# The attention state of the first twelve tiles: added on TensorE through an identity and copied by ScalarE instead of added on VectorE, with the first loads in another order

## The chip, the cores and the metric

The kernel runs on one core of a Trainium2 chip. Its time is the device time of one execution in microseconds (us), and the smaller is the better. Five engines work side by side, each through its own queue in order: TensorE (PE in the rows, its weight loads PEld), VectorE (DVE), ScalarE (ACT), GpSimd (POOL) and SyncE (SP), which issues nearly all transfers (DMA).

## The reference

Three layers, one after the other, on 3072 tokens of 512 channels. The change lies in the first.

```python
# attention: B=4 sequences, H=8 heads, S=768, head size 64
state = zeros((B, H, D, D))
for t in range(S):
    state = gamma * state + k[:, :, t] (outer) v[:, :, t]
    y[:, :, t] = scale * q[:, :, t] @ state
# x = y as (3072, 512)
h = x @ w_in;  x = (max(h, 0) + alpha * min(h, 0)) @ w_out      # dense layer, 2048 wide
# expert layer: 8 experts of 1024; each token goes to one expert
out[t] = gate[t] * (max(x[t] @ w1[e], 0) @ w2[e])
```

The inputs are float32, and the result has to be about that exact. The kernel therefore splits operands into two float16 halves (high and low) and multiplies with three products, or it multiplies in float32.

## The kernel before

**Tiles.** The 3072 tokens are 24 tiles of 128: tile `i` is chunk `c = i // 4` of sequence `b = i % 4`. The recurrence is done by chunks: within a tile by masked scores, across tiles by a state per sequence. The state lies in `st_bd[:, b]`, as four 128x128 blocks of which only the two 64x64 blocks on the diagonal are used; the rest stays at zero from a memset.

**What one tile does** (lines 476 to 610):

- `att_load` issues the loads on SP's queue: `qk_t[i]` (q, k by channel and k by token, 768 KB), `v_t[i]` (256 KB), and for every fourth tile the decay factors `cqk_sb` of its chunk (512 KB: one half for q, one for k).
- `att_hat` multiplies q (and, for tiles from `HALVED = 12` on, k) by the factors on VectorE. For tiles below 12 only the q half of `cqk_sb` is read, and v is scaled instead of k.
- `att_a` makes the scores on TensorE in float32, and VectorE masks them with `cau`.
- `att_b` multiplies scores by v and q by the state into the PSUM bank `y`, then k by v into the PSUM bank `u` (128x512), both in float32 for tiles below 12. ScalarE sums the squares of `y`, VectorE derives a scale, ScalarE and VectorE write the two halves `xh`. Last, two VectorE additions (64x256 each) add the diagonal blocks of `u` into `st_bd`. The last chunk of a sequence needs no state.

`y` and `u` come from `m_ring`, which has two banks, handed out in the order of the program; the small sums over partitions (`total`) take their bank from it too.

**The first stretch** also has to prepare the dense layer: `convert` unpacks `w_in` and `w_out` (three ScalarE and two VectorE operations of 1024 columns for each of sixteen pieces), `quarter` and `split_out` split them in halves, and `mm1` / `mm2` multiply. `mm1(0, m)`, the first batch of four tiles, starts as soon as quarter 0 of `w_in` is split, so it is mixed with tiles 4 to 11 and with the rest of the unpacking. Each `mm1` takes a bank of `h_ring` (two) that ScalarE and VectorE empty into `g` and from there into two float16 halves.

**The order of work.** No engine's order is written by hand. Every instruction is recorded by `Plan` (lines 97 to 323) with an estimated duration from `cost`, and `issue` runs a list scheduler over the record: it decides from the estimates in which order each engine, and SP's transfers, get their instructions. All instructions are then emitted by line 147, which is why all rows name that line. Changing an estimate can move instructions on any engine, in the whole kernel.

Of the kernel before, what the change touches and what calls it, by code (L numbers as in the profile page):

```python
# [14 lines left out]
AF = mybir.ActivationFunctionType  # L15
ALU = mybir.AluOpType
AX = mybir.AxisListType

B, H, S, D = 4, 8, 768, 64
NT, DM, DFF = B * S, H * D, 2048  # L20
E, F = 8, 1024
P = 128
# [74 lines left out]
class Plan:  # L97
# [37 lines left out]
    class Engine:  # L135
# [26 lines left out]
        def cost(self, method, kw):  # L162

            n = 1
            for d in kw["out"].shape[1:]:
                n *= d
            if "dma" in method:
                side = kw["in_"] if "indirect" not in method or kw["in_offset"] is None else kw["out"]
                n = 1
                for d in side.shape:  # L170
                    n *= d
                nb = n * mybir.dt.size(side.dtype)
                if "indirect" in method:
                    return 1040.0, 650.0, nb
                return 60.0, (1150.0 if "transpose" in method else 1000.0), nb * (1.23 if "transpose" in method else 1)
            if self.name == "PE":
                if kw["lhsT"].dtype == F32:
                    return max(214.0, 1.67 * n), 0.0, 0
                return max(27.0, 0.416 * n + 2.5), 0.0, 0
            if self.name == "ACT":  # L180
                extra = sum(93.0 for k in ("accum_out", "scale", "bias") if isinstance(kw.get(k), bass.AP))
                return (95.0 if kw["in_"].space != bass.MemoryType.PSUM else 50.0) + 0.833 * n + extra, 0.0, 0
            if self.name == "DVE":
                fast = method in ("tensor_scalar", "tensor_copy") and n > 64 and kw.get("op0") not in self.BITS
                two = method in ("scalar_tensor_tensor", "tensor_tensor") and n > 256
                return 65.0 + n * (0.52 if fast else 1.05) * (1.15 if two else 1.0), 0.0, 0
            return 140.0 + (2.13 if method == "tensor_tensor" else 1.3) * n, 0.0, 0
# [139 lines left out]
def retention_prelu_moe_kernel(ctx: ExitStack, tc, qkv, w_in, w_out, alpha, emb, tau, w1, w2,  # L327
# [3 lines left out]
    V, A, G, T, SP = plan.vector, plan.scalar, plan.gpsimd, plan.tensor, plan.sync  # L331
# [10 lines left out]
    def buf(name, shape, dt=F32):  # L342
        return sbuf.tile([P, *shape], dt, name=name, tag=name)
# [12 lines left out]
    def tmp(name, shape, dt=F32, n=2):  # L356
        if name not in small:
            small[name] = Ring([buf(f"{name}_{k}", shape, dt) for k in range(n)])
        return small[name].next()
# [2 lines left out]
    cst = buf("cst", [NCOL])  # L362
    cst16 = buf("cst16", [2 * P + E], F16)
    cau = buf("cau", [P])
    alpha_sb = buf("alpha_sb", [KF])
    tau_sb = buf("tau_sb", [1])
    cqk_sb = buf("cqk_sb", [2, KD, P])

    def col(name):
        return cst[:, _COLS[name][0]:_COLS[name][1]]  # L370

    tri, ones16, base16 = cst16[:, 0:P], cst16[:, P:2 * P], cst16[:, 2 * P:]
# [14 lines left out]
    v_ring = Ring([vp_buf[:, k] for k in range(2)])  # L387
# [4 lines left out]
    first = {"qk": [room[:, 1536 * k:1536 * k + 1536].rearrange("p (a x) -> p a x", a=3) for k in range(3)] + [qk_buf, hat_buf, stage[:, 12:15]],  # L392
             "v": [room[:, 4608 + 512 * k:5120 + 512 * k] for k in range(2)] + v_ring.bufs,
             "pm": [room[:, 5632 + 512 * k:6144 + 512 * k].rearrange("p (k t) -> p k t", k=KD) for k in range(4)] + pm_ring.bufs,
             "xh": [room[:, 7680 + 512 * k:8192 + 512 * k].bitcast(F16).rearrange("p (a x) -> p a x", a=2) for k in range(3)] + xh_ring.bufs,
             }
    first = {k: Ring(v) for k, v in first.items()}
# [28 lines left out]
    def pow2(ss, s, c, hb=None):  # L426

        if hb is None:
            hb = tmp(f"hb{ss.shape[1]}", [ss.shape[1]], I32)
        V.tensor_scalar(out=hb, in0=ss.bitcast(I32), scalar1=0x7F000000, scalar2=1,  # L430
                        op0=ALU.bitwise_and, op1=ALU.logical_shift_right)
        V.tensor_scalar(out=s.bitcast(I32), in0=hb, scalar1=-1, scalar2=c << 23, op0=ALU.mult, op1=ALU.add)
        return hb

    def pow2_inverse(hb, i, c):
        V.tensor_scalar(out=i.bitcast(I32), in0=hb, scalar1=(254 - c) << 23, scalar2=None, op0=ALU.add)
# [9 lines left out]
    def square_sum(src, acc, junk):  # L446
        A.activation(out=junk, in_=src, func=AF.Square, accum_out=acc)
# [25 lines left out]
    N_ROOM = 2  # L473
    qk_t, v_t, att = {}, {}, {}

    def att_load(i):
        if i % B == 0:
            SP.dma_start(out=cqk_sb, in_=cqk[i // B])
        qk_t[i] = (first["qk"] if i < B * N_ROOM else qk_ring).next() if i < HALVED else qk_buf
        SP.dma_start(out=qk_t[i], in_=qkv[i, :, 0:3])  # L480
        v_t[i] = (first["v"] if i < B * N_ROOM else v_ring).next()
        SP.dma_start(out=v_t[i], in_=qkv[i, :, 3])

    def att_hat(i):
# [40 lines left out]
    HALVED = 12  # L525
# [36 lines left out]
    def att_b(i, early=False):  # L562

        c, b = divmod(i, B)
        j, o = divmod(i, BT)
        v = v_t.pop(i)
        hat, pr = att.pop(i)
        st = st_bd[:, b]
        y = m_ring.next()
        with plan.unit("PE"):  # L570
            for p in range(KD):
                for r in range(2):
                    h = 2 * p + r
                    if i >= HALVED:
                        for n, (a, o_) in enumerate(((0, 0), (0, 1), (1, 0))):
                            T.matmul(out=y[:, D * h:D * h + D], lhsT=p16[r][:, a, P * p:P * p + P],
                                     rhs=v16[:, o_, D * h:D * h + D], start=(r == n == 0), stop=False, skip_group_check=True)
                        continue
                    T.matmul(out=y[:, D * h:D * h + D], lhsT=pr[r][:, p, :], rhs=v[:, D * h:D * h + D],
                             start=(r == 0), stop=(r == 1 and not c), skip_group_check=True)  # L580
                if c:
                    T.matmul(out=y[:, P * p:P * p + P], lhsT=hat[:, 0, P * p:P * p + P], rhs=(st_y if i >= HALVED else st)[:, p, :],
                             start=False, stop=True, skip_group_check=True)
        if c < NCH - 1:
            u = m_ring.next().rearrange("p (k t) -> p k t", k=KD)
            with plan.unit("PE"):
                for p in range(KD):
                    T.matmul(out=u[:, p, :], lhsT=hat[:, 2, P * p:P * p + P], rhs=v[:, P * p:P * p + P],
                             start=True, stop=True)
        xh = (first["xh"] if i < B * N_ROOM else xh_ring).next()  # L590
        ss = tmp("ssx", [1])
        square_sum(y, ss, xh[:, 0, :])
        if c < NCH - 1:
            for r in (0, D):
                V.tensor_tensor(out=st[r:r + D, :, r:r + D], in0=u[r:r + D, :, r:r + D],
                                in1=st[r:r + D, :, r:r + D], op=ALU.add)
        s = tmp("sx", [1])
        pow2(ss, s, C_WIDE, hbx[:, i:i + 1])
        if o == BT - 1:
            pow2_inverse(hbx[:, i + 1 - BT:i + 1], invx[:, i + 1 - BT:i + 1], C_WIDE)  # L600
            for k in range(i + 1 - BT, i + 1):
                if k in y_inv:
                    for q in range(2):
                        V.tensor_tensor(out=invx[:, k:k + 1], in0=invx[:, k:k + 1], in1=y_inv[k][:, q:q + 1], op=ALU.mult)
        A.activation(out=xh[:, 0, :], in_=y, func=AF.Copy, scale=s)
        V.scalar_tensor_tensor(out=xh[:, 1, :], in0=y, scalar=s, in1=xh[:, 0, :], op0=ALU.mult, op1=ALU.subtract)
        if early:
            SP.dma_start(out=x_dram[i], in_=xh.rearrange("p a x -> p (a x)"))
        else:
            att_x(i, xh.rearrange("p a x -> p (a x)"))  # L610
# [376 lines left out]
    SP.dma_start(out=tau_sb, in_=tau.partition_broadcast(P))  # L987
    SP.dma_start(out=emb_sb, in_=emb)
    V.memset(st_bd, 0.0)
    V.memset(csum, 0.0)  # L990
    V.memset(ss_b, 0.0)
    V.memset(ones_b, 1.0)
# [40 lines left out]
    for i in range(2 * B, NTILE):  # L1033
        c, b = divmod(i, B)
        s = KF * (c - 1) + 3 * b
        early = i < first_late
        if not early:
            k = 2 + int((i - first_late) * 4.5)
            early = k < KF * (c - 2) + 14
            k = min(k, s)  # L1040
# [18 lines left out]
    for s in range(NS + BT + 12):  # L1059
# [5 lines left out]
        for o in range(BT - 1, -1, -1):  # L1065
            n = s - o
            if n >= NS - KF:
                n = max(s - LAG[o], NS - KF - 1)
# [6 lines left out]
            if m == KF - 1:  # L1075
                i = BT * j + o
                if j < NB - 1:
                    if o == 0:
                        routes[j] = Route(i, BT)
                    r = routes[j]  # L1080
# [8 lines left out]
                else:  # L1089
                    r = Route(i, 1)  # L1090
# [8 lines left out]
    def sl(shape, dt=F32):  # L1099
# [3 lines left out]
        if dt != F32:  # L1103
# [24 lines left out]
                    in1=ntl.unsqueeze(1).to_broadcast([P, E, E]), op=ALU.mult)  # L1128
# [7 lines left out]
                    in1=cum[:, 0:E - 1].unsqueeze(1).to_broadcast([P, SL, E - 1]), op=ALU.is_ge)  # L1136
# [220 lines left out]
```

## Time and profile before

| | |
|---|---|
| median of 3 runs | 981.19 us (980.25 to 981.85) |
| the profiled execution | 988.65 us |
| its span, first to last instruction | 986.9 us |
| outside the span | 1.75 us |
| TensorE busy | 926.3 us, 94% of the span |
| VectorE busy | 571.3 us, 58% |
| ScalarE busy | 464.6 us, 47% |
| TensorE's mean granted clock | 0.966 |

The durations of the rows come from the profiled execution, which took 7.46 us more than the median run. Shares over the whole span hide that the kernel has two parts with different limits: a first one in which TensorE often waits, and a long one in which it hardly does.

### The profile page before, as it was taken

To read this page: it belongs to the slowest core of one execution; us is meant where nothing else is said; L and a number is where in the kernel's file an instruction comes from. 1 tells how busy PE (TensorE), PEld (TensorE's weight loads), DVE (VectorE), ACT (ScalarE), POOL (GpSimd) and SP (SyncE) were. 2 spreads that over 40 slices of the span, in tenths; PEclk is the share of its full clock that TensorE was granted. 3 is DMA by queue.
4 is the path that set the end of the run, shared out by engine and by line. 5 is a ranking of instruction groups with operands and counts; after the bars stand their busy time and mean duration, and the time that the engine had idled before them with its cause. 6 is when DMAs were issued, how large, how long until landed. Compare 5 with 4: busy or idle time off the path is not lost. (4 is left out here: it accounts for less than half of the span.)

```text
span 986.9 us, 18868 instructions
## 1 busy us (share of the span) xinstructions
PE 926.3 (94%) x7100; PEld 558.7 (57%) x7100; DVE 571.3 (58%) x1490; ACT 464.6 (47%) x825; POOL 91.4 (9%) x110
## 2 busy tenths in 40 slices
PE   6797789999999999999998999997999999989995
PEld 6775455555555555554444444446677677666663
DVE  5988989578787877796466557446422222121231
ACT  1568866577687778887576664222001101100100
POOL 0000000000200010001000100110232112132010
PEclk9797979999999999999999999998999999989998
DMA  9998723564899888888686543797687279945450
GB/s 306 305 266 254 239 102 89 161 159 119 261 277 233 221 269 269 235 229 291 197 236 229 192 156 100 298 261 153 219 195 188 72 222 341 311 114 111 63 196 25
DMA packets 129823, 201.44 MB, mean 204 GB/s; under 512 B 89726, under 2 KB 90110, under 8 KB 124608
## 3 DMA queue, kind: packets, MB, share of 16 engines
q1 hardware_dynamic: 123168, 179.42, 62.1%
q0 software_dynamic: 6560, 20.77, 6.5%
q8 instruction: 57, 0.93, 0.4%
q14 instruction: 38, 0.31, 0.1%
HBM read 200.40 MB, written 51.14 MB: 255 GB/s over the span
## 5 line engine op out<-in xcount | busy, mean ns | idle before, releaser
L147 PE MATMUL bank<-xT,win 128*128 128x512 f16 x1152 | 270.7, 386 | 7.0 <-DVE g L147 7.0
L147 PE MATMUL bank<-wout,f_buf 128*128 128x512 f16 x960 | 223.4, 381 | 0.8 <-DVE pay_buf L147 0.8
L147 PEld LDWEIGHTS <-win 128*128 128x128 f16 x1344 | 123.3, 100 | 136.9 <-issue 15.7
L147 PEld LDWEIGHTS <-f_buf 128*128 128x128 f16 x960 | 93.1, 98 | 110.9 <-issue 4.0
L147 PEld LDWEIGHTS <-stage 128*128 128x128 f16 x1440 | 89.3, 98 | 26.8 <-issue 4.2
L147 DVE SCALAR_TENSOR_TENSOR g<-g,oma,bank 128x512 f32<-128x512 f32 x96 | 71.4, 745 | 55.3 <-ACT g L147 54.6
L147 ACT ACTIVATE wout<-stage 128x1024 f16<-128x1024 f32 x64 | 67.3, 1052 | 39.2 <-DMA stage<-in_w 38.6
L147 ACT ACTIVATE st_bd<-bank 128x512 f16<-128x512 f32 x30 | 17.9, 597 | 140.5 <-PE bank L147 126.8
L147 ACT ACTIVATE g<-bank 128x512 f32<-128x512 f32 x96 | 56.4, 588 | 57.0 <-PE bank L147 56.7
L147 DVE SCALAR_TENSOR_TENSOR f_buf<-g,f_buf 128x512 f16<-128x512 f32 x80 | 55.1, 689 | 32.9 <-ACT f_buf L147 32.4
L147 POOL DMA_INDIRECT table<-pay_buf,rposi x24 | 25.6, 1066 | 473.3 <-DVE v L147 112.7
L147 PEld LDWEIGHTS <-wout 128*128 128x128 f16 x1152 | 65.9, 98 | 5.2 <-issue 2.2
L147 PEld LDWEIGHTS <-st_bd 128*128 128x128 f16 x408 | 39.8, 99 | 47.6 <-issue 2.5
L147 ACT ACTIVATE f_buf<-g 128x512 f16<-128x512 f32 x80 | 49.8, 623 | 29.0 <-DVE g L147 28.9
L147 DVE SCALAR_TENSOR_TENSOR stage<-stage,se 128x1024 f16<-128x1024 f32 x43 | 55.0, 1280 | 8.4 <-ACT stage L147 8.4
L147 PE MATMUL bank<-xT,stage 128*128 128x128 f16 x960 | 56.8, 220 | 3.2 <-issue 3.2
L147 PE MATMUL bank<-xT,wout 128*128 128x128 f16 x960 | 56.5, 220 | 1.8 <-issue 1.8
L147 DVE SCALAR_TENSOR_TENSOR st_bd<-bank,st_bd 128x512 f16<-128x512 f32 x34 | 23.3, 689 | 55.0 <-ACT st_bd L147 50.3
L147 ACT ACTIVATE stage<-stage,se 128x1024 f16<-128x1024 f32 x43 | 48.8, 1139 | 9.6 <-DMA wsplit<-stage 5.7
L147 DVE TENSOR_SCALAR xT<-bank,f_buf,cqk_sb 128x512 f32<-128x512 f32 x20 | 16.2, 810 | 62.4 <-PE bank L147 62.4
L147 PEld LDWEIGHTS <-x2T_buf 128*128 128x128 f16 x384 | 26.9, 99 | 34.1 <-DMA x2T_buf<-pay_buf 8.0
L147 PE MATMUL bank<-wout,stage 128*128 128x512 f16 (+1 forms) x200 | 44.6, 375 | 0.0
(263 smaller groups left out, 1257.8 us busy)
## 6 DMA issues: line engine op xcount, KB each, us to landing
stage<-wsplit SPq DMA_DIRECT2D x52, 1024.0 KB
wout<-wsplit SPq DMA_DIRECT2D x52, 1024.0 KB
stage<-in_w SPq DMA_DIRECT2D x64, 512.0 KB
wsplit<-stage SPq DMA_DIRECT2D x43, 512.0 KB
qk_buf<-in_qkv SPq DMA_DIRECT2D x15, 768.0 KB
wsplit<-win SPq DMA_DIRECT2D x21, 512.0 KB
f_buf<-in_w_in SPq DMA_DIRECT2D x12, 512.0 KB
vp_buf<-in_qkv SPq DMA_DIRECT2D x20, 256.0 KB
```

The source lines that it names most:

```text
L147: call = lambda: fn(**kw)
```

## The change

Four things are changed.

1. **State.** For tiles 4 to 11 TensorE first multiplies an identity matrix by the old state into the whole of `u` (one float32 matmul, 128x512), and k by v is accumulated on top of it. For tiles 0 to 3 nothing is added, as the state is zero. For all twelve tiles ScalarE then copies the two diagonal parts of `u` into `st_bd`; VectorE's additions remain for tiles 12 to 19.
2. **Identity.** A new buffer `ident` is made once on VectorE, as the difference of the two masks `cau` and `tri`.
3. **First loads.** Below tile 12 only the q half of `cqk_sb` is loaded (256 KB less, three times). For tile 0 the loads are issued in smaller pieces: q and k by channel, the factors, v, and k by token last.
4. **Estimates.** The planner's cost of a float32 matmul is replaced: 145 ns for 64 rows, and 120 ns + 1.17 ns per column else, in place of 1.67 ns per column and at least 214 ns.

```diff
                 if kw["lhsT"].dtype == F32:
-                    return max(214.0, 1.67 * n), 0.0, 0
+                    rows, cols = kw["lhsT"].shape[0], kw["lhsT"].shape[1]
+                    return (145.0 if rows < P else 100.0 if cols < P else 120.0 + 1.17 * n), 0.0, 0
...
+    ident = buf("ident", [P])
...
     def att_load(i):
-        if i % B == 0:
-            SP.dma_start(out=cqk_sb, in_=cqk[i // B])
+        if i % B == 0 and i:
+
+            n = 1 if i < HALVED else 2
+            SP.dma_start(out=cqk_sb[:, 0:n], in_=cqk[i // B][:, 0:n])
         qk_t[i] = (first["qk"] if i < B * N_ROOM else qk_ring).next() if i < HALVED else qk_buf
+        v_t[i] = (first["v"] if i < B * N_ROOM else v_ring).next()
+        if i == 0:
+
+            SP.dma_start(out=qk_t[i][:, 0:2], in_=qkv[i, :, 0:2])
+            SP.dma_start(out=cqk_sb[:, 0:1], in_=cqk[0][:, 0:1])
+            SP.dma_start(out=v_t[i], in_=qkv[i, :, 3])
+            SP.dma_start(out=qk_t[i][:, 2], in_=qkv[i, :, 2])
+            return
         SP.dma_start(out=qk_t[i], in_=qkv[i, :, 0:3])
-        v_t[i] = (first["v"] if i < B * N_ROOM else v_ring).next()
         SP.dma_start(out=v_t[i], in_=qkv[i, :, 3])
...
             with plan.unit("PE"):
+
+                add = 0 < c and i < HALVED
+                if add:
+                    T.matmul(out=u.rearrange("p k t -> p (k t)"), lhsT=ident, rhs=st.rearrange("p k t -> p (k t)"),
+                             start=True, stop=False, skip_group_check=True)
                 for p in range(KD):
                     T.matmul(out=u[:, p, :], lhsT=hat[:, 2, P * p:P * p + P], rhs=v[:, P * p:P * p + P],
-                             start=True, stop=True)
+                             start=not add, stop=True, skip_group_check=True)
...
             for r in (0, D):
-                V.tensor_tensor(out=st[r:r + D, :, r:r + D], in0=u[r:r + D, :, r:r + D],
-                                in1=st[r:r + D, :, r:r + D], op=ALU.add)
+                if i < HALVED:
+                    A.activation(out=st[r:r + D, :, r:r + D], in_=u[r:r + D, :, r:r + D], func=AF.Copy)
+                else:
+                    V.tensor_tensor(out=st[r:r + D, :, r:r + D], in0=u[r:r + D, :, r:r + D],
+                                    in1=st[r:r + D, :, r:r + D], op=ALU.add)
...
     V.memset(st_bd, 0.0)
+    V.tensor_tensor(out=ident, in0=cau, in1=tri, op=ALU.subtract)
```

## Rows read from the trace of the kernel before

**Rows 1.** Busy time by stretch: columns are stretch, length, engines, granted clock, DMA share, GB/s.

```profile
0.00:140.00 140.00, 108.14 (x704) 82.47 (x705) 115.69 (x198) 89.28 (x133) 0.81 (x8) 0.88 0.80 256
140.00:987.00 847.00, 818.14 (x6397) 476.21 (x6395) 455.65 (x1292) 375.36 (x693) 90.61 (x102) 0.98 0.67 195
```

**Rows 2.** The same by shorter stretches; engines in the order PE, PEld, DVE, ACT, POOL.

```profile
0.00:24.00 24.00, 15.21 (x96) 14.25 (x97) 12.40 (x27) 4.70 (x6) 0.39 (x5) 1.00 0.92 308
24.00:48.00 24.00, 18.76 (x150) 17.29 (x149) 21.00 (x43) 12.83 (x21) 0.00 (x0) 0.79 0.97 299
48.00:73.00 25.00, 24.40 (x192) 18.46 (x192) 21.01 (x35) 15.79 (x26) 0.00 (x0) 1.00 0.96 283
...
80.00:88.00 8.00, 7.39 (x33) 7.08 (x34) 6.77 (x13) 6.97 (x10) 0.00 (x0) 0.50 0.74 231
76.00:140.00 64.00, 49.57 (x268) 32.45 (x269) 58.31 (x91) 53.03 (x80) 0.42 (x3) 0.83 0.68 222
```

**Rows 3.** Waits of TensorE, 0 to 147 us: total, times, longest.

```profile
PE bank L147 <- DVE wout L147: 14.5, 6, 7.7
PE bank L147 <- DVE xh L147: 8.3, 3, 5.1
PE bank L147 <- DVE g L147: 7.0, 3, 4.4
```

**Rows 4.** Timeline of the start: start, length, engine, operation, idle before and its releaser.

```profile
0.75 0.40 SPq L147 DMA_DIRECT2D wout<-in_qkv  x1
1.20 0.42 SPq L147 DMA_DIRECT2D cqk_sb<-in_cqk  x1
...
6.99 0.69 DVE L147 TENSOR_TENSOR wout<-wout,cqk_sb 128x512 f32<-128x512 f32 x1 [3.82 <-DMA cqk_sb<-in_cqk]
...
7.73 2.08 PE L147 MATMUL bank<-wout 64*128 64x128 f32 x16 [7.73 <-DVE wout L147]
...
10.12 0.69 DVE L147 TENSOR_TENSOR wout<-wout,cqk_sb 128x512 f32<-128x512 f32 x1 [1.30 <-DMA wout<-in_qkv]
```

**Rows 5.** Groups of ScalarE, 0 to 130 us, shapes apart: busy, mean ns.

```profile
L147 ACT ACTIVATE g<-bank 128x512 f32<-128x512 f32 x11 | 6.5, 587 | 3.9 <-PE bank L147 3.9
L147 ACT ACTIVATE f_buf<-win 128x1024 f16<-128x1024 f32 x6 | 6.3, 1054 | 2.9 <-DVE win L147 2.8
```

**Rows 6.** The state tile: durations in ns (least, median, most), first and last start.

```profile
L147 DVE TENSOR_TENSOR st_bd<-bank,st_bd x24: 404/427/456, 18.8 to 147.0; 64x256 f32<-64x256 f32 x24
```

**Rows 7.** Timeline of TensorE, 48 to 66 us: records in a row, two for each float32 matmul.

```profile
51.38 1.06 PE L147 MATMUL bank<-wout,stage 128*128 128x128 f32 x8
52.28 5.34 PE L147 MATMUL bank<-xT,win 128*128 128x512 f16 x24
...
62.32 2.75 PE L147 MATMUL bank<-xT,win 128*128 128x512 f16 x12
64.91 0.55 PE L147 MATMUL bank<-vp_buf,wout 128*128 128x64 f32 x4
```

**Rows 8.** Timeline of all engines, 68 to 79 us.

```profile
67.81 0.83 PE L147 MATMUL bank<-vp_buf,wout 128*128 128x128 f32 x6
...
68.22 1.15 ACT L147 ACTIVATE win<-f_buf 128x1024 f32<-128x1024 f32 x1 [2.52 <-DMA f_buf<-in_w_in]
...
72.36 0.60 ACT L147 ACTIVATE xh<-bank 128x512 f16<-128x512 f32 x1
...
77.48 0.74 DVE L147 SCALAR_TENSOR_TENSOR xh<-bank,sx,xh 128x512 f16<-128x512 f32 x1
...
78.27 0.58 PE L147 MATMUL bank<-accw,cst 128*128 128x2 f32 x2 [5.06 <-DVE xh L147]
```

**Rows 9.** Timeline of TensorE, 80 to 88 us.

```profile
80.61 2.07 PE L147 MATMUL bank<-vp_buf,qk_buf 128*128 128x128 f32 x8 [1.75 <-DVE tot L147]
82.48 0.95 PE L147 MATMUL bank<-vp_buf 128*128 128x64 f32 x4
```

**Rows 10.** Timeline of TensorE around 139 us.

```profile
139.27 2.29 PE L147 MATMUL bank<-xT,win 128*128 128x512 f16 x5 [1.69 <-DVE g L147]
```

## The prediction

> **What bounds the kernel now.** I read the table of busy time by stretch first. From 140 us to the end TensorE works 818 of 847 us, and in the first 140 us only 108.1 [rows 1]. So the kernel has two parts. The long one has TensorE as its limit: work added to TensorE there, or an instruction taken from VectorE there, would be paid in full or bring nothing. The first part has 140 - 108.1 = 31.9 us in which TensorE waits, and all four parts of the change lie in it, except for the estimates of the planner.
>
> The second view is the list of what TensorE waits for. Nearly all of the 31.9 us ends on VectorE: 14.5 us on operands that VectorE writes, 8.3 on the two halves `xh`, 7.0 on `g` [rows 3]. That names the last link only, so the third view is the shorter stretches. Until about 73 us the transfers are as busy as TensorE and VectorE (shares 0.92, 0.97, 0.96), at 283 to 308 GB/s. From 76 to 140 us VectorE is busy for 58.3 of 64 us and ScalarE for 53.0, TensorE for 49.6 [rows 2]. So the transfers and the chains of a tile share the limit at first, then VectorE with ScalarE close behind. TensorE leaves this regime at 139.27 us, after a last wait for VectorE's `g` [rows 10].
>
> The fourth view is the granted clock. Where TensorE waited 5.06 us [rows 8] the stretch behind it, 80 to 88 us, was granted 0.50, the lower of the two levels [rows 2]: there four float32 matmuls of 128 columns take 82.48 - 80.61 = 1.87 us [rows 9], at the upper level 52.28 - 51.38 = 0.90 [rows 7]. A wait in this kernel is thus paid a second time.
>
> The sum is made against the profiled execution, 988.65 us (986.9 of span and 1.75 around it); it lies 7.46 us above the median of 981.19, and I carry the difference in microseconds over to the median.
>
> **The change, part by part.**
>
> *First loads.* TensorE's first matmul starts at 7.73 us, behind VectorE's multiplication by the factors, which waited 3.82 us for them [rows 4]. Ahead of it 768 + 512 KB had to arrive; afterwards 512 + 256 KB, so 512 KB less, which at 308 GB/s [rows 2] is 1.7 us. Tile 1's operands, for which VectorE waits next (at 10.12 us, the masks of tile 0 behind it in its queue) [rows 4], have only the k half of the factors, 256 KB, less ahead of them: 0.85 us. The fourth issue for tile 0 costs SP some 0.4 us [rows 4], while transfers already queued are moving. Bounds 0 to -1.7; I take -0.85, since tile 1's wait comes last. The Trainium skill (DMA: Bandwidth & Descriptors, section Measured) advises transfers of 1 MiB or more, and so speaks against cutting the load in pieces; by that rule this term would be about 0. This trace moves 308 GB/s in its first 24 us with transfers that are all below 1 MiB, so I don't follow it here.
>
> *The two later factor loads* are 256 KB smaller each, 0.9 us at 283 to 299 GB/s, in stretches where the transfers are 96% busy [rows 2]. A late transfer is what held ScalarE at 68.22 us [rows 8]. Bounds 0 to -1.8; I take one of the two, -0.9.
>
> *VectorE* loses 24 additions of 427 ns [rows 6], 10.2 us. It gains one subtraction 128x128 for the identity, below the 0.69 us of the 128x512 one [rows 4], made before tile 4 wants it; I count it as nothing, hidden by VectorE's idle time in the first 24 us (12.4 of 24 busy), and as 0.7 without that cover. Four pairs, 3.4 us, lie in 76 to 140 us, where VectorE has 5.7 us left of 64 [rows 2]. There the bounds are 0 and -3.4; I take -2.4, nearer the full value, as TensorE's waits end on VectorE. Eight pairs, 6.8 us, belong to tiles 0 to 7, where a chain over three engines and the transfers share the limit: bounds 0 and -6.8, taken -2.0.
>
> *ScalarE* gains 24 copies 64x256. The trace has none; the rows nearest are 587 ns at 512 columns and 1054 at 1024 [rows 5], 0.91 ns a column, so about 0.35 us at 256: 8.5 us in all, 2.8 of them in the four tiles of 76 to 140 us. That makes ScalarE 53.0 + 2.8 = 55.8 there and VectorE 58.3 - 3.4 = 54.9: level. Each copy waits in ScalarE's queue for TensorE's `u`; behind it stand the unpacking, the square of `y` and the emptying of `g`, for which VectorE and then `mm1`'s banks wait. Bounds 0 and +8.5; I take +1.3, as 0.83 of ScalarE's time there is taken and most of the copies fit between.
>
> *TensorE* gains eight float32 matmuls of 512 columns, which the trace doesn't have either. Four of 128 columns take 0.90 us, 0.225 each, and a float16 one of 512 columns takes (64.91 - 62.32) / 12 = 0.216 [rows 7]: so one float32 column costs what four float16 ones do, and the identity 0.86 us. Eight are 6.9 us at the upper clock, twice that at the lower; a lower bound is two records of 0.216 each, 3.5 us. Where do they fall? Tiles 6 and 7 run in a stretch without gaps (24.4 of 25 us) [rows 2], but what follows it is the wait to 78.27 us, and that one ends on `xh` of tile 7, whose `y` ScalarE read only at 72.36 us while TensorE was already at the tile's `u` at 67.81 [rows 8]: some 4 us of room, more than the 1.7 added. Tiles 8 to 11 lie among 64 - 49.6 = 14.4 us of waits. So most of it is covered by waits of TensorE; the bounds are 0 and +6.9, and I take +1.0, for the tile at the lower clock.
>
> *Estimates.* The matmuls themselves are unchanged. The new estimates (270 ns in place of 214 for a 128x128 one, which takes 225 in a row of four [rows 7]) can reorder everything. No row prices that; I take 0 and leave it to the rivals.
>
> Sum: -0.85 - 0.9 - 2.4 - 2.0 + 1.3 + 1.0 = -3.85 us. That is 984.8 in a profiled execution, and 981.19 - 3.85 = 977.3 as the median. Another way to see it: TensorE's idle time and slow stretches in the first part must shrink by 6.9 us for no change at all, and by 10.8 for this forecast; 31.9 are there.
>
> **Rivals.**
>
> 1. *The waits are too short for the clock to fall* (faster still). The stretch at 0.50 from 80 to 88 us does 7.39 us of work [rows 2] that would take 3.7 at the upper level. If the waits ahead of it and ahead of the last one at 139 us [rows 10] are gone, some 2 x 3.7 = 7.4 us come on top: 969.9. For it: TensorE's added work itself fills waits. Against it: the wait to 78.27 us hangs on `xh` and on a bank, which the change doesn't free.
> 2. *The load only changes engines* (no change). VectorE and ScalarE come out level in 76 to 140 us and each waits for the other; what is gained at the start is paid by the identity: 981, within 0.2% (2 us, about what a measurement of this kernel can tell).
> 3. *ScalarE becomes the last* (slower). Place: 76 to 140 us. The copies stand ahead of the emptying of `g`; their 2.8 us and the four identities there, 3.5 us, are paid in full, and of the gains only the loads' 1.75 remain: +4.55, 985.7. It decides from where ScalarE is busier than VectorE in that stretch, by my sum 55.8 against 54.9, so it is near. The Trainium skill (ScalarE: Activation LUTs, Rules for kernel authors) says to use VectorE, not ScalarE, for simple element operations; by that rule the copies are a loss. By this trace's rows one copy (0.35) is not dearer than one addition (0.427), so the rule alone doesn't bear here.
> 4. *The planner's new order is worse* (slower): one more wait like that of 5.06 us [rows 8], with the 3.7 us of slow clock behind it, less the sum: +4.9, 986.1. Against it: the same planner, with the same margins, made the present order, whose long waits are few.
>
> **How the numbers follow.** The forecast, with a range of its own of 974.5 to 979, gets 0.46; rival 1 gets 0.13, rival 2 0.17, rival 3 0.16 and rival 4 0.08. So faster by over 0.2% is 0.59, within it 0.17, slower 0.24. The range reaches to about the price of rivals 1 and 4, each with a part of its chance left outside: 969 to 986.
>
> **What would show it.** Right: TensorE's first matmul near 6 us; VectorE's busy time down by about 10 us in the first 150 us, ScalarE's up by 8 to 9; identity matmuls of about 0.86 us; TensorE's last long wait ending some 4 us sooner than 139.27 us, and the same work after it. Wrong, if ScalarE's busy share from 76 to 140 us is above VectorE's and `mm1` waits for banks that ScalarE empties; if the identities run at the lower clock (1.7 us each); if TensorE's waits behind 140 us grow from the 28.9 us of now [rows 1]; or if the order of tiles and `mm1` on TensorE in the first part is another.

## The result, and the profile after

The changed kernel takes 975.22 us in the median of 20 runs, the kernel before 983.9 in 20 runs beside them: ratio 0.9914, 95% interval 0.9894 to 0.9935, which is 8.5 us faster (6.4 to 10.4). One of the 20 runs of the changed kernel took 1917 us, with no cause shown, and is left out of the ratio, as is one of 1587 us of the kernel before beside the first four experiments. The forecast was 3.85 us faster (977.3 after 981.19). The direction and the range held; the gain is more than twice the one forecast.

The two profiled executions differ by more, 986.9 against 972.9 us of span. They are single executions: the one before, 988.65 us, lies 4.75 above the median of its 20 runs, the one after, 974.65, 0.57 below. So some 5 of the 14 us are a matter of which execution was profiled, and the rows below tell where time went, not how much was gained. In every table of busy time the columns are the stretch, its length, the engines PE, PEld, DVE, ACT and POOL with their instruction counts, granted clock, DMA share and GB/s.

Busy time by stretch of the changed kernel:

```profile
0.00:24.00 24.00, 16.01 (x92) 14.82 (x94) 12.86 (x28) 5.59 (x9) 0.39 (x5) 1.00 0.97 323
24.00:48.00 24.00, 20.04 (x165) 18.46 (x166) 19.73 (x39) 17.77 (x32) 0.00 (x0) 0.91 1.00 309
48.00:73.00 25.00, 25.00 (x151) 18.24 (x151) 16.96 (x25) 13.73 (x24) 0.00 (x0) 0.88 0.84 218
...
76.00:140.00 64.00, 52.99 (x308) 34.10 (x306) 54.96 (x85) 54.85 (x86) 1.11 (x3) 0.92 0.70 218
0.00:140.00 140.00, 117.05 (x735) 87.46 (x736) 106.96 (x178) 94.95 (x153) 1.50 (x8) 0.93 0.82 252
140.00:973.00 833.00, 808.63 (x6383) 470.95 (x6380) 454.69 (x1290) 377.23 (x697) 91.92 (x102) 0.99 0.67 199
```

In the first 140 us TensorE now idles for 140 - 117.05 = 22.95 us, against 31.9 [rows 1], although it has the identities to do as well. Behind 140 us it idles for 24.4, against 28.9, and has 808.6 us of work left there, against 818.1. VectorE and ScalarE are level from 76 to 140 us, 54.96 and 54.85, as the sum had it (54.9 and 55.8).

Waits of TensorE in the first 147 us:

```profile
PE bank L147 <- DVE wout L147: 11.9, 4, 7.2
PE bank L147 <- DVE xh L147: 4.3, 2, 3.1
PE bank L147 <- DVE g L147: 3.3, 2, 3.0
PE bank L147 <- ACT f_buf L147: 2.1, 1, 2.1
PE bank L147 <- DVE vp_buf L147: 1.1, 1, 1.1
PE bank L147 <- ACT st_bd L147: 1.1, 1, 1.1
```

The three waits on VectorE of [rows 3] fell from 29.8 us to 19.5. New are two on ScalarE, 3.2 us: one is the bank `u` of tile 11, which the copies of tile 10 still hold (the wait ends at 133.63 us, just behind them).

The new instructions, from the state's and the identity's views (ns: least, median, most; first and last start in us):

```profile
L147 ACT ACTIVATE st_bd<-bank x24: 357/378/380, 23.9 to 140.4; 64x256 f32<-64x256 f32 x24
...
L147 PE MATMUL bank<-st_bd,ident x16: 592/594/1061, 41.5 to 134.2; 128*128 128x512 f32 x16
L147 DVE TENSOR_TENSOR ident<-cau,cst x1: 279/279/279, 25.6 to 25.6; 128x128 f32<-128x128 f32 x1
```

Sixteen records are eight identities, each in two passes that overlap; what one costs is read from start to start. TensorE's timeline from 7 us on:

```profile
7.21 2.08 PE L147 MATMUL bank<-wout 64*128 64x128 f32 x16 [7.21 <-DVE wout L147]
10.06 5.86 PE L147 MATMUL bank<-wout 128*128 128x64 f32 x32 [0.78 <-DVE wout L147]
15.85 0.59 PE L147 MATMUL bank<-am,cst 128*128 128x1 f32 x2
16.37 7.49 PE L147 MATMUL bank<-wout 64*128 64x128 f32 x40
...
41.52 1.02 PE L147 MATMUL bank<-st_bd,ident 128*128 128x512 f32 x2
42.38 1.05 PE L147 MATMUL bank<-wout,hat_buf 128*128 128x128 f32 x8
43.36 1.16 PE L147 MATMUL bank<-wout 64*128 64x128 f32 x16
...
51.33 1.91 PE L147 MATMUL bank<-st_bd,ident 128*128 128x512 f32 x2
53.04 1.46 PE L147 MATMUL bank<-wout,stage 128*128 128x128 f32 x8
...
84.74 1.92 PE L147 MATMUL bank<-st_bd,ident 128*128 128x512 f32 x2
86.44 1.81 PE L147 MATMUL bank<-vp_buf,qk_buf 128*128 128x128 f32 x8
...
143.01 0.39 PE L147 MATMUL bank<-accw,cst 128*128 128x8 f32 x2 [2.10 <-ACT f_buf L147]
```

The first identity costs 42.38 - 41.52 = 0.86 us. Two of the eight, at 51.33 and 84.74 us, cost twice that, 1.71 and 1.70; the stretch from 80 to 88 us, behind a wait of 3.15 us, was granted 0.57. Two things are to be seen at the start: the first matmul comes only 0.52 us sooner than in [rows 4], and what follows it is another order. The product of tile 0 with v (128x64) now stands ahead of tile 1's scores (64x128), where before tile 1's scores came next. No row of before could show that: the new estimates did it, as the experiments show.

### The profile page after: what moved, and what is told of

It is laid out like the page before. It is cut to its first block, busy times and chain, and to the rows that moved or that the text cites. A ratio compares the mean times of both kernels' runs of the same rounds, so it can differ in the third digit from the quotient of the medians.

```text
span 972.9 us, 18898 instructions
## 1 busy us (share of the span) xinstructions
PE 925.7 (95%) x7116; PEld 558.4 (57%) x7116; DVE 561.6 (58%) x1467; ACT 472.2 (49%) x849; POOL 93.4 (10%) x110
## 5 line engine op out<-in xcount | busy, mean ns | idle before, releaser
L147 PE MATMUL bank<-xT,win 128*128 128x512 f16 x1152 | 265.2, 381 | 4.1 <-DVE g L147 3.3
L147 PEld LDWEIGHTS <-stage 128*128 128x128 f16 x1440 | 88.9, 98 | 24.7 <-issue 1.9
L147 ACT ACTIVATE st_bd<-bank 128x512 f16<-128x512 f32 (+1 forms) x54 | 26.9, 498 | 139.2 <-PE bank L147 135.5
L147 ACT ACTIVATE x2T_buf<-bank 128x512 f16<-128x512 f32 x14 | 8.4, 597 | 75.9 <-PE bank L147 61.2
L147 PE MATMUL bank<-wout,st_bd 128*128 128x512 f16 x192 | 44.2, 388 | 1.0 <-issue 1.0
```

The lines of the kernel that those rows point to most:

```text
L147: call = lambda: fn(**kw)
```

## The experiments

Thirteen kernels, the changed one among them, each experiment against runs of the kernel before on the same chip. An experiment has 12 executions, no_loads and identity_twice 6. The microseconds are (ratio - 1) x 984, about the median of the kernel before; 95% intervals in brackets.

| kernel | state | loads | estimates | ratio | us |
|---|---|---|---|---|---|
| changed kernel | new | new | new | 0.9914 [0.9894, 0.9935] | -8.5 |
| state_only | new | old | old | 1.0005 [0.998, 1.003] | +0.5 |
| loads_only | old | new | old | 1.0023 [1.0, 1.0046] | +2.3 |
| costs_only | old | old | new | 0.9975 [0.9945, 1.0005] | -2.5 |
| no_costs | new | new | old | 1.0015 [0.9986, 1.0043] | +1.5 |
| no_loads | new | old | new | 0.9903 [0.9867, 0.9939] | -9.5 |
| no_state | old | new | new | 0.9966 [0.9937, 0.9996] | -3.3 |
| identity_twice | new, identity doubled | new | new | 0.9899 [0.9862, 0.9937] | -9.9 |
| copies_on_vector | new, copies on VectorE | new | new | 0.9937 [0.9909, 0.9966] | -6.2 |
| copies_twice | new, copies doubled | new | new | 0.9979 [0.9953, 1.0005] | -2.1 |
| state_early | new | old | new for the scores of tiles 0 to 3 alone | 0.9987 [0.996, 1.0015] | -1.3 |
| state_late | new | old | new but for these | 0.9958 [0.9935, 0.998] | -4.1 |
| early_only | old | old | new for the scores of tiles 0 to 3 alone | 1.0036 [1.0015, 1.0058] | +3.5 |

**Each part alone, and the whole without the estimates.** Theory S was the prediction's: the state's move off VectorE is the cause. Against it stood E, the estimates, and L, the loads. The edits put the old lines back, as here for the estimates (state_only against no_loads, no_costs against the changed kernel):

```diff
-                    rows, cols = kw["lhsT"].shape[0], kw["lhsT"].shape[1]
-                    return (145.0 if rows < P else 100.0 if cols < P else 120.0 + 1.17 * n), 0.0, 0
+                    return max(214.0, 1.67 * n), 0.0, 0
```

> Parts 1 and 2 of the change alone (identity on TensorE, copies on ScalarE), with the old loads and the old estimates. Theory S, the state's move off VectorE is what shortens TensorE's waits: most of the change's 8.7 us, so 5 to 8 us faster than before, and TensorE's idle time in the first 140 us down from 31.9 to about 25. Theory E, the new estimates and the order they make are the cause: 0 to 2 us faster or even slower, as 6.9 us of work come on top. Theory L, the loads are the cause: within 2 us of before.

> Part 3 alone (smaller factor loads, tile 0 in pieces). Theory S: 1 to 2 us faster, as the sum of the prediction has it (0.85 + 0.9). Theory L: 4 us or more faster. Theory E: within 2 us.

> Part 4 alone: only the planner's estimates of float32 matmuls, so the same instructions in another order. Theory S: within 3 us of before, either way. Theory E: 4 us or more faster, and the waits behind 140 us (28.9 us before, 24.4 after) shorter too.

> The whole change without part 4: state and loads with the old estimates. Theory S: 6 to 9 us faster than before, about the changed kernel. Theory E: at most 4 us faster. Theory L: as theory S, so it doesn't tell these two apart; state_only and loads_only do.

Theory S fell as it stood: the state alone moves nothing, +0.5. L fell too, +2.3. The estimates alone gave 2.5 us with an interval that touches no change, so E isn't borne out either; but without them the rest of the change gives nothing, +1.5.

The trace of state_only shows how easily one would have been misled:

```profile
0.00:140.00 140.00, 115.29 (x703) 84.36 (x704) 102.60 (x175) 93.63 (x148) 0.39 (x5) 0.90 0.80 254
140.00:990.00 850.00, 815.14 (x6415) 476.01 (x6413) 459.64 (x1293) 380.22 (x702) 96.04 (x105) 0.99 0.66 195
```

TensorE's idle time in the first 140 us is 24.7 us, as theory S expected (about 25), and its span, 980.0 us, is 6.9 below the one before. Its 12 executions together show no gain at all: 983.76 us in the median, 984.56 before. The shorter waits were filled with the identities' 6.9 us, and the difference of the spans is a matter of which executions happened to be profiled.

**The other two pairs.** In no_loads and no_state one part is taken back and the estimates stay. The edit of no_state, in `att_b`:

```diff
-                add = 0 < c and i < HALVED
-                if add:
-                    T.matmul(out=u.rearrange("p k t -> p (k t)"), lhsT=ident, rhs=st.rearrange("p k t -> p (k t)"),
-                             start=True, stop=False, skip_group_check=True)
...
-                if i < HALVED:
-                    A.activation(out=st[r:r + D, :, r:r + D], in_=u[r:r + D, :, r:r + D], func=AF.Copy)
-                else:
-                    V.tensor_tensor(...)
+                V.tensor_tensor(out=st[r:r + D, :, r:r + D], in0=u[r:r + D, :, r:r + D],
+                                in1=st[r:r + D, :, r:r + D], op=ALU.add)
```

> State and estimates (parts 1, 2 and 4) with the old loads. Theory S has fallen as it stood, since the state alone moved nothing. Theory I, the state's move pays only when the planner's estimates let it place the float32 matmuls well: 6 to 9 us faster than before. Theory L2, the loads are needed too: at most 4 us faster.

> Loads and estimates (parts 3 and 4) with the state on VectorE as before. Theory I: about what the estimates alone gave, 1 to 4 us faster. Theory E, the estimates' order with the loads is all that counts: 7 us or more faster. Theory L2: in between, 4 to 6.

Theory I, state and estimates together, holds: 9.5 us without the loads. The state is worth 7.0 us with the new estimates (-9.5 against -2.5) and nothing with the old ones (+0.5 against 0); with the new loads these are 5.2 and 0.8. The estimates are worth 10 us with the state moved and 2.5 without; with the new loads 10 and 5.6. What state and estimates give beyond their sum is thus 7.5 and 4.4 us; from the intervals of the table I estimate each to within 5, so that only the first is clear of nothing by itself. The loads are worth nothing in any of four pairs: +2.3, +1.0, -0.8, +1.0.

**The price of each engine's part.** The identity issued twice (the second writes the same again), the copies put on VectorE, and the copies issued twice:

```diff
+                    T.matmul(out=u.rearrange("p k t -> p (k t)"), lhsT=ident, rhs=st.rearrange("p k t -> p (k t)"),
+                             start=True, stop=False, skip_group_check=True)
```

```diff
-                    A.activation(out=st[r:r + D, :, r:r + D], in_=u[r:r + D, :, r:r + D], func=AF.Copy)
+                    V.tensor_copy(out=st[r:r + D, :, r:r + D], in_=u[r:r + D, :, r:r + D])
```

```diff
+                    A.activation(out=st[r:r + D, :, r:r + D], in_=u[r:r + D, :, r:r + D], func=AF.Copy)
```

> The changed kernel with each of the eight identity matmuls issued twice in a row, the second writing the same over the first; the result is the same. 6.9 us more work on TensorE at the upper clock. If the identity is covered by TensorE's waits in the first part: within 2 us of the changed kernel. If TensorE is the limit there: 5 to 8 us slower than the changed kernel. The planner's estimates can move the order in both cases.

> The changed kernel with the 24 state copies on VectorE instead of ScalarE; everything else is the same. Theory I with VectorE as the limit of the first part: most of the gain is lost, 4 to 8 us slower than the changed kernel. If the relief of VectorE is worth nothing: within 2 us of the changed kernel.

> The changed kernel with each of the 24 state copies on ScalarE issued twice in a row, the second writing the same: 24 x 0.378 = 9.1 us more on ScalarE. If ScalarE has room in the first part: within 2 us of the changed kernel. If it is level with VectorE there, as the prediction's sum has it: 3 to 8 us slower than the changed kernel.

Another 6.9 us on TensorE cost nothing that shows: 9.9 us faster than before, against 8.5 for the changed kernel (the difference to within about 4, an estimate from the two intervals). In its trace the identities fill waits, and what is idle falls again:

```profile
0.00:140.00 140.00, 119.33 (x763) 84.61 (x764) 110.99 (x185) 99.31 (x161) 3.11 (x8) 0.95 0.79 252
```

Another 9.1 us on ScalarE cost 6.4 us (0.9979 - 0.9914). Its trace shows where: from 76 to 140 us ScalarE has 59.26 us of 64 and is now ahead of VectorE, and TensorE's waits for `xh`, which ScalarE writes first, are back:

```profile
76.00:140.00 64.00, 50.79 (x301) 33.71 (x300) 54.81 (x87) 59.26 (x94) 1.01 (x3) 0.90 0.70 226
```

```profile
PE bank L147 <- DVE xh L147: 7.8, 3, 5.0
PE bank L147 <- DVE g L147: 5.4, 4, 2.2
```

The copies on VectorE cost 2.3 us, with overlapping intervals; the expectation, 4 to 8, was too high, and no change isn't excluded. Its page says more:

```profile
PE 927.3 (95%) x7116; PEld 559.8 (57%) x7116; DVE 570.8 (58%) x1491; ACT 464.1 (47%) x825; POOL 94.9 (10%) x110
```

VectorE and ScalarE are as busy there as in the kernel before (571.3 and 464.6 us), and 6.2 of the 8.5 us remain. So the relief of VectorE, the prediction's largest term, isn't shown to be what the state's move is worth.

**Where in the order the estimates work.** TensorE's timeline in state_only and in no_loads, which differ in the estimates alone:

```profile
7.71 2.08 PE L147 MATMUL bank<-wout 64*128 64x128 f32 x16 [7.71 <-DVE wout L147]
11.23 2.08 PE L147 MATMUL bank<-wout 64*128 64x128 f32 x16 [1.44 <-DVE wout L147]
13.23 0.58 PE L147 MATMUL bank<-am,cst 128*128 128x1 f32 x2
13.68 12.89 PE L147 MATMUL bank<-wout 128*128 128x64 f32 x64
...
35.14 3.68 PE L147 MATMUL bank<-vp_buf,wout 128*128 128x64 f32 x16 [3.18 <-DVE wout L147]
...
43.86 0.38 PE L147 MATMUL bank<-accw,cst 128*128 128x2 f32 x2
```

```profile
7.66 2.08 PE L147 MATMUL bank<-wout 64*128 64x128 f32 x16 [7.66 <-DVE wout L147]
10.52 5.86 PE L147 MATMUL bank<-wout 128*128 128x64 f32 x32 [0.78 <-DVE wout L147]
...
32.64 2.00 PE L147 MATMUL bank<-vp_buf,wout 128*128 128x64 f32 x16 [0.34 <-DVE wout L147]
...
37.60 0.38 PE L147 MATMUL bank<-accw,cst 128*128 128x2 f32 x2 [0.87 <-DVE xh L147]
```

With the old estimates tile 1's scores come first and tile 0's product with v starts at 13.68 us, with the new ones at 10.52. Tile 3's product waits 3.18 us for VectorE against 0.34, and the sum for quarter 0 of `w_in` comes at 43.86 us against 37.60 (at 40.94 in the kernel before). Theory O took this one choice at the start for the whole cause. The test changes one estimate, for four tiles:

```diff
+                    if kw["lhsT"].shape[0] < P and self.plan.first_tiles:
+                        return 145.0, 0.0, 0
                     return max(214.0, 1.67 * n), 0.0, 0
...
+    plan.first_tiles = False
     quarter(0)
```

state_late has the same condition with 214.0 in front of the new estimates, early_only is state_early without the state's move.

> state_only, which moved nothing, with one estimate changed: 145 ns instead of 214 for the 64-row matmuls (the scores) of tiles 0 to 3 alone. That makes the planner put tile 0's product with v ahead of tile 1's scores on TensorE, as in the changed kernel. Theory O, this one order at the start is what the state's move needs, since every later tile waits for the bank of the one before: 6 to 9 us faster than before. Theory R, the estimates work through the rest of the order: within 3 us of before.

> The complement: state and all new estimates with the old loads (no_loads, 9.5 us faster than before), except that the 64-row matmuls of tiles 0 to 3 keep 214 ns, so tile 1's scores stand ahead of tile 0's product with v as before. Theory O: the gain is mostly gone, within 3 us of before. Theory R: 6 to 9 us faster.

> The kernel before (state added on VectorE) with only the estimate of state_early. Theory O: the tiles' chain starts 3 us sooner, but VectorE takes it back: 1 to 4 us faster, as the estimates alone gave. If the order at the start were all: 6 to 9 us faster. Theory R: within 2 us.

Theory O fell. In state_early the order at the start is the changed kernel's, tile 0's product starts at 10.48 us (the edit adds a line, so 147 becomes 148):

```profile
10.48 5.86 PE L148 MATMUL bank<-wout 128*128 128x64 f32 x32 [0.78 <-DVE wout L148]
...
40.28 0.58 PE L148 MATMUL bank<-accw,cst 128*128 128x2 f32 x2
```

Of the 6.3 us at quarter 0's sum 3.6 are won (40.28), but the median gains only 1.3, within no change. With the state on VectorE (early_only) the same order is 3.5 us slower than before, which none of its expectations had. The complement keeps 4.1 us. Nor does the time of that sum follow the gain: in state_late it comes at 37.92 us, nearly as early as in no_loads, with less than half the gain. Neither half has the whole. 1.3 + 4.1 = 5.4 is less than 9.5, but by the three intervals the halves may still just add up. So the first choice doesn't carry the gain alone, and which of the later ones do stays open.

**What the estimates change on TensorE.** A part of the answer stands in the pages of the two pairs that differ in the estimates alone, with the state moved: state_only and no_loads, then no_costs and the changed kernel.

```profile
PE 930.4 (95%) x7116; PEld 560.4 (57%) x7116; DVE 562.2 (57%) x1467; ACT 473.8 (48%) x849; POOL 96.4 (10%) x110
PE 923.6 (95%) x7116; PEld 557.1 (57%) x7116; DVE 561.5 (58%) x1467; ACT 471.8 (49%) x849; POOL 96.7 (10%) x110
...
PE 932.3 (95%) x7116; PEld 559.6 (57%) x7116; DVE 561.7 (57%) x1467; ACT 473.6 (48%) x849; POOL 96.2 (10%) x110
PE 925.7 (95%) x7116; PEld 558.4 (57%) x7116; DVE 561.6 (58%) x1467; ACT 472.2 (49%) x849; POOL 93.4 (10%) x110
```

The spans are 980.0, 970.7, 981.4 and 972.9 us. For the same 7116 instructions TensorE is busy 6.8 and 6.6 us less with the new estimates, while its idle time falls only from 49.6 to 47.1 and from 49.1 to 47.2. The granted clock goes with it: over all executions its mean is 0.977 with the old estimates and 0.981 and 0.982 with the new. A difference of 0.0045 to 0.005 of some 980 us is 4 to 5 us: by that estimate, an upper one, since TensorE is idle in a part of the time at the lower clock, up to half of the 10 us is the clock. So the new order gains in good part because the same work takes less time, and not by shorter waits alone. How the order does that isn't shown; and the clock alone isn't the gain, since it rises from 0.967 to 0.977 with the state alone (state_only), which gains nothing.

## Why the prediction was right, and where it was wrong

That the time came out in the range, and on the side that was forecast, is in part luck. The sum got its gain from VectorE and the loads and put the estimates at 0; without the new estimates the same change measures 1.5 us slower, which can't be told from no change.

**What bounds the kernel: right.** The gain lies where TensorE waited, in the first 140 us for the larger part, and doubling TensorE's added work cost nothing that shows there.

**TensorE's term, +1.0: right in kind.** The identity was worked out at 0.86 us and took 0.86, at the lower clock 1.7 (two of eight). A second set cost nothing that shows (identity_twice), so the term is about 0.

**ScalarE's term, +1.3: not measured by itself.** The copy was worked out at 0.35 us and took 0.378. What is shown is that there is little room beyond the first set: a second one cost 6.4 us for 9.1. Rival 3 named the place, 76 to 140 us, and a point from which it decides, ScalarE busier than VectorE. The changed kernel stands just short of it (54.85 against 54.96), copies_twice beyond it (59.26 against 54.81). But the point itself isn't borne out: in no_loads, 9.5 us faster than before, ScalarE is the busier there too, 55.53 against 54.25:

```profile
76.00:140.00 64.00, 52.87 (x295) 33.57 (x295) 54.25 (x88) 55.53 (x90) 1.11 (x3) 0.92 0.68 215
```

The Trainium skill's rule (ScalarE: Activation LUTs, Rules for kernel authors) sends `relu`, `max`, `min`, `add` and `mul` to VectorE; a plain copy isn't among them. This kernel isn't faster with the copies on VectorE (2.3 us slower, with overlapping intervals).

**The loads' two terms, -0.85 and -0.9: wrong.** They measured nothing. The first matmul came 0.52 us sooner, not 1.7, and tile 1's operands, on which the -0.85 rested, are no longer what TensorE waits for, as tile 0's product with v goes ahead. With the old order they don't come sooner either. Tile 1's scores in the kernel before, then in loads_only:

```profile
10.87 2.08 PE L147 MATMUL bank<-wout 64*128 64x128 f32 x16 [1.06 <-DVE wout L147]
...
11.57 2.08 PE L147 MATMUL bank<-wout 64*128 64x128 f32 x16 [2.35 <-DVE wout L147]
```

The Trainium skill's advice on transfers of 1 MiB (DMA: Bandwidth & Descriptors, section Measured) would have made this term 0; that it came out so is no proof of the rule, since the first 24 us moved 323 GB/s with the smaller pieces.

**VectorE's term, -4.4: not borne out as a term.** The work moved about as counted: 571.3 to 561.6 us, ScalarE 464.6 to 472.2 (of the four pairs counted into 76 to 140 us, tile 11's ran behind it, at 145.89 and 146.99). With the old estimates it brought nothing; with the new ones the state's move as a whole brought 5.2 to 7.0 where the three terms of VectorE, ScalarE and TensorE sum to -2.1. The relief of VectorE itself measured 2.3 us, with no change not excluded (copies_on_vector).

**The estimates, "I take 0 and leave it to the rivals": the step that failed.** They were looked at only as a risk (rival 4, slower), with 0.08. They are worth 2.5 us alone, within noise, and 10 with the state moved, which without them gives nothing. The old estimate for a score matmul was 214 ns. In the trace of the kernel before, the eight of a tile (16 records) start at 60.23 us and the next group at 61.32:

```profile
60.23 1.16 PE L147 MATMUL bank<-wout 64*128 64x128 f32 x16
61.32 1.16 PE L147 MATMUL bank<-vp_buf,wout 128*128 128x128 f32 x8
```

That is 0.136 us each, and the new 145 ns is close to it. The prediction compared the new estimate only for the 128x128 matmul, where 270 is further from the 225 ns than the old 214, and missed the scores. For the 128x512 identity the new estimate is the worse one too, 719 ns against 855 for the 860 measured. So not every new figure is a better one, and which of them carries the gain isn't shown beyond state_early and state_late.

**The sign of the other rivals.** Rival 1, more gain because the clock stays up, came true in part: the mean granted clock is 0.976 to 0.985 in the 19 executions of the changed kernel that count, and 0.961 to 0.977 in the 92 of the kernel before beside the experiments. In the profiled pair TensorE's busy time is 925.7 us against 926.3 with 6.9 us more to do, so the higher clock about pays for the identities, and 13.4 of the 14.0 us are idle time. Rival 2, no change, is what the change is without part 4.

**The signs it named.** VectorE's busy time and the identity's 0.86 us came as said. TensorE's first matmul came at 7.21 us and not near 6, and its last wait of the first part ends on ScalarE at 143.01 us, not some 4 us before 139.27. Two signs of being wrong were met: another order on TensorE, and identities at the lower clock, two of eight.

## What to carry to other kernels

Where a planner orders the work, a change of its estimates is a change of the kernel: price it by comparing old and new estimate with the rows of each operation it concerns, and test it alone and with the rest, because neither part may show what the two give together. Doubling an instruction that writes the same again is a cheap test of whether an engine has room: here it told TensorE's free time from ScalarE's, which busy shares of 77% and 83% from 76 to 140 us before the change didn't. And one pair of profiles isn't a result: in state_only it showed 6.9 us that 12 runs against 34 don't.

## What the runs showed of the hardware beyond that

TensorE took 2.08 us for the 16 records of a tile's scores (float32, 64 rows) at 7.21 us, although the granted clock is shown as 1.00 there, and 1.16 us for 16 such records at 43.36 us; so it worked at little more than half its later speed in the first stretch, while the column shows the full clock there. Why isn't shown. Equal kernels spread more than expected: the 20 runs of the kernel before reach from 979.8 to 987.91 us, so that 3 runs, which the forecast started from (981.19), were 2.7 us off the median of 20.
